# A transformer block on one core: GpSimd's and SP's order inside the attention blocks, and the steps behind the last maximum

## The chip, the core and the metric

The kernel runs on one core of one Trainium2 chip. The metric is the device time of one execution in microseconds (us), taken as the median of three runs. A profile of one execution, with a trace of every instruction, goes with it. TensorE (PE) multiplies matrices, VectorE (DVE), ScalarE (ACT) and GpSimd (POOL) work element by element, and SyncE (SP) only issues transfers; its queue is called SPq in the trace. Each engine takes its own instructions strictly in the order in which they stand, and waits for the others by semaphores.

## The reference

A block of a transformer on 2048 rows of 576 numbers, in float32: layer norm, attention with 32 heads of 18 numbers each, a residual, a second layer norm, a gated feed-forward part with 4608 inner columns, a residual.

```python
qkv = (x_normed @ wqkv).reshape(B, S, 3, H, Dh) ...      # H = 32, Dh = 18
scores = jnp.einsum("bhqd,bhkd->bhqk", q, k) * scale
p = _softmax(scores, axis=-1)
o = jnp.einsum("bhqk,bhkd->bhqd", p, v)
h = x + o.reshape(B, S, D) @ wo
g, u = layernorm(h) @ w_gate, layernorm(h) @ w_up
h2 = h + (gelu(g) * u) @ w_down
```

## The kernel before

Products in float32 accuracy are made of float16 ones: each number is split into a high and a low part, and the products high-high, high-low and low-high are added in PSUM.

**Attention.** The 32 heads are worked in 8 groups of 4 (`NG`), the queries in 4 pieces of 512 (`NB`). A *block* n is one group with one piece of queries, 32 blocks in all (`NS`); n // 4 is the group g and n % 4 the piece qc. A block has 16 *steps* kt, one for each 128 keys. In a step `score` (L704) multiplies 128 keys with 512 queries for the four heads into PSUM banks, ScalarE takes the exponential (L714 for two heads at once, L716 for one), and `weigh` (L725) multiplies the exponentials of the step before with V in two halves of 256 queries, each half called "w". The array is used in tiles of 64 rows by 32 columns: heads 0 and 2 lie in rows 0 to 63, heads 1 and 3 in rows 64 to 127.

**Maxima.** Each query's largest score has to be subtracted before the exponential. `maxima` is a generator that runs one and a half blocks ahead: 64 units a block, each a product of 128 queries with 512 keys (L642), whose maximum VectorE takes (L656, and L654 for pairs of key blocks that are compared by key differences). When a block's 64 units are done and the generator is resumed once more, `max_finish` reduces them (L667), GpSimd scales them and splits them into two parts (L670 to L672), SP transposes these (L674) and writes them as two more rows of the stacked queries Q in four transfers (L680). The scores of that block read Q, and so wait for it.

**Behind a block.** `out_block` has three parts, run at steps of the next block. First (step 0 or 1): ScalarE copies the sums out of PSUM (L739), GpSimd adds the second bank (L742), SP fetches the row sums (rc, L747). Second (step 3): GpSimd makes their reciprocals (L754 to L758), and SP sends them out and back spread over the rows (L762, L763). Third (step 5, or 6 in the last blocks): GpSimd multiplies and splits (L767 to L769), and SP copies the result into the activations X (L782, L785, L786). From block 30 on VectorE does the multiplying.

**Loads.** `load_stacks` brings the next group's queries and keys (L593, L594; 12 transfers on SP, 12 on GpSimd), `load_ends` the keys of which `key_steps` makes the differences (GpSimd L622 to L625, SP L628 and L630). They stand at steps 2 and 9 of a group's first block (of the second block in group 0).

**What sets the order.** The order of the main loop is written out by hand: `STEPS` holds two strings, for even and odd steps, in which "s23" scores heads 2 in bank 3, "S010" heads 0 and 1 in banks 0 and 1, "m4" or "o2" resumes `maxima` once in that bank, "w" weighs a half, and "f" takes a piece of work that is done on the side. `in_order` keeps TensorE, ScalarE, VectorE and GpSimd to the order in which the program issues. SP is not kept to it in the main loop: a scheduler places SP's transfers, until the second `in_order` behind the loop.

**Behind the last maximum.** Maxima end at step 489 of 512 (`LAST_MAX`, block 30, step 9). From there on `STEPS` runs with "m" doing nothing, and each step takes a half of an output product: `wo_pairs` multiplies 128 rows with 288 columns of wo in 14 matmuls (L325, from `accumulate`) into one bank, VectorE adds x and stores the row (L859), whose statistics follow (L213, L214, and GpSimd's L250 to L258). `rows0` makes from pairs of such rows the sums and splits that the feed-forward part multiplies (L261, GpSimd L908 to L911, VectorE L917 to L921), and SP transposes them into X and V (L947). It is taken twice a step from the ninth step on. A third set of 512 rows follows in eight halves, seven of them behind the loop, through four banks; then the first unit of the feed-forward part starts (L1193).

## Time and profile before

| | us |
|---|---|
| median of 3 runs | 2631.65 (2628.14 to 2634.61) |
| the profiled execution | 2628.84 |
| its span in the trace | 2627.1 |
| TensorE busy | 2548.7 (97%) |
| VectorE busy | 2003.7 (76%) |
| ScalarE busy | 1651.6 (63%) |
| GpSimd busy | 858.0 (33%) |

The span is the time from the first to the last instruction; the execution has 1.7 us around it. Busy times are shares of the whole span, in which three stretches follow each other: the preparation to about 200 us, the attention to about 1405 us, the feed-forward part to the end. In a row of the trace stand the start, the duration, the engine, the line, the operation, the tiles written and read with their sizes, the count, and in brackets how long the engine stood idle before and what ended that.

### The profile page before, as it was taken

The numbers are of one execution on the slowest core, as the hardware profiler recorded it, in microseconds if no ns is written. First come the engines' busy times: TensorE is split into PE (matmuls) and PEld (weight loads), VectorE is DVE, ScalarE is ACT, GpSimd is POOL, SyncE is SP. The second block draws the span as 40 slices with busy tenths as digits, with TensorE's granted clock in tenths as the row PEclk, the third lists the DMA queues.
The fourth block names the chain that finished last, engine by engine and source line by source line (L and its number), as shares of the span: only waits on it lengthen the run. The fifth ranks groups of instructions, "written<-read, shape, count | busy, mean of one in ns | idle before, by whom it ended". The sixth has DMA issues, their size and how long they took to land.

```text
span 2627.1 us, 96403 instructions
## 1 busy us (share of the span) xinstructions
PE 2548.7 (97%) x41245; PEld 1446.6 (55%) x41245; DVE 2003.7 (76%) x3888; ACT 1651.6 (63%) x2898; POOL 858.0 (33%) x1176
## 2 busy tenths in 40 slices
PE   8999899999999999999999999999999999999999
PEld 4645455555555555555555555555555555555555
DVE  8479899999999999999957765656565656565653
ACT  6229899999999999999965433333333333333332
POOL 4301532332323232433676432222222222222221
PEclk9999999999999999999999999999999999999999
DMA  8621010101101010101126410101010101011110
GB/s 225 153 78 46 18 47 21 43 19 32 36 18 44 18 47 21 44 20 30 29 59 130 91 34 30 34 30 34 30 34 30 34 30 34 30 33 31 33 56 36
DMA packets 170367, 120.96 MB, mean 46 GB/s; under 512 B 88664, under 2 KB 147564, under 8 KB 169938
## 3 DMA queue, kind: packets, MB, share of 16 engines
q1 hardware_dynamic: 161198, 98.47, 14.0%
q0 software_dynamic: 8608, 16.33, 2.4%
q8 instruction: 322, 5.28, 0.9%
q14 instruction: 107, 0.88, 0.1%
q10 hardware_dynamic: 132, 0.01, 0.0%
HBM read 80.05 MB, written 15.01 MB: 36 GB/s over the span
## 4 chain that ended last, share of the span: by engine, by line
PE 67%; DVE 8%; POOL 7%; issue 5%; SPq 5%; ACT 4%; DMA 4%; ACTq 0%; POOLq 0%; DVEq 0%
PE bank L1193 14%; PE more L1193 14%; PE bank L325 11%; PE more L325 8%; DVE mx L656 6%; PE bank L642 4%; ACT WK L716 3%; PE bank L725 3%; PE quad L725 3%; PE quad L325 2%; DVE nat L654 2%; PE pair L704 2%; POOL rp L754 2%; PE bank L704 1%; SPq L628 1%
## 5 line engine op out<-in xcount | busy, mean ns | idle before, releaser
L656 DVE TENSOR_REDUCE mx<-bank 128x1 f32<-128x512 f32 x1064 | 707.9, 683 | 61.9 <-PE bank L642 60.3
L725 PE MATMUL bank<-WK,V 64*32 64x256 f32 x8192 | 644.8, 383 | 11.0 <-ACT nat L739 10.5
L725 PE MATMUL quad<-WK,V 64*32 64x256 f32 x8192 | 644.2, 383 | 0.2 <-DVE nat L744 0.2
L716 ACT ACTIVATE WK<-bank 128x512 f32<-128x512 f32 x768 | 530.7, 691 | 49.4 <-PE bank L642 33.3
L1193 PEld LDWEIGHTS <-W 128*128 128x128 f16 x2394 | 234.0, 98 | 278.5
L325 PEld LDWEIGHTS <-WK 128*128 128x128 f16 x3456 | 338.2, 98 | 88.3
L716 ACT ACTIVATE WK<-quad 128x512 f32<-128x512 f32 x512 | 355.4, 694 | 16.2 <-PE bank L704 12.7
L656 DVE TENSOR_REDUCE mx<-pair 128x1 f32<-128x512 f32 x488 | 336.8, 690 | 2.9 <-PE pair L642 0.8
L714 ACT ACTIVATE WK<-pair 128x1024 f32<-128x1024 f32 x256 | 279.5, 1092 | 0.4 <-ACT WK L716 0.2
L725 PEld LDWEIGHTS quad<-WK,V 64*32 64x32 f32 x8192 | 239.5, 106 | 29.5 <-DVE nat L744 0.7
L725 PEld LDWEIGHTS bank<-WK,V 64*32 64x32 f32 x8192 | 220.4, 106 | 39.2 <-ACT nat L739 21.4
L325 PE MATMUL more<-W,WK 128*128 128x288 f16 x1728 | 235.2, 286 | 0.0
L325 PE MATMUL bank<-W,WK 128*128 128x288 f16 x1728 | 235.2, 286 | 0.0
L642 PEld LDWEIGHTS <-W 54*32 54x32 f16 x4096 | 139.3, 90 | 171.4 <-issue 111.4
L642 PEld LDWEIGHTS <-A 54*32 54x32 f16 x4096 | 131.7, 90 | 169.8 <-issue 112.5
L1193 PE MATMUL bank<-X,W 128*128 128x512 f16 x792 | 223.8, 379 | 0.0
L642 PE MATMUL bank<-W 54*32 54x512 f16 x2048 | 206.4, 389 | 6.0
L642 PE MATMUL bank<-A 54*32 54x512 f16 x2220 | 205.2, 387 | 6.1 <-DVE mx L656 0.4
L1061 POOL TENSOR_TENSOR A<-A 128x384 f32<-128x384 f32 x136 | 138.5, 1039 | 200.9 <-DMA A<-in_B_w_up_dram 117.1
L1193 PE MATMUL bank<-V,W 128*128 128x512 f16 x720 | 202.4, 379 | 0.0
L1207 POOL TENSOR_TENSOR WK<-tmp,WK 128x512 f16<-128x512 f32 x73 | 88.7, 1215 | 307.5 <-ACT WK L1204 307.2
L716 ACT ACTIVATE WK<-pair 128x512 f32<-128x512 f32 x256 | 178.6, 698 | 0.0
(360 smaller groups left out, 4952.8 us busy)
## 6 DMA issues: line engine op xcount, KB each, us to landing
A<-in_B_w_down_dram SPq DMA_DIRECT2D x8, 1152.0 KB
nat<-rc SPq DMA_DIRECT2D x32, 256.0 KB
A<-in_B_w_gate_dram SPq DMA_DIRECT2D x64, 128.0 KB
A<-in_B_w_up_dram SPq DMA_DIRECT2D x64, 128.0 KB
qk_hi<-tmp SPq DMA_DIRECT2D x36, 128.0 KB
qk_lo<-tmp SPq DMA_DIRECT2D x36, 128.0 KB
out_dram<-nat SPq DMA_DIRECT2D x16, 288.0 KB
X<-nat SPq DMA_DIRECT2D x100, 36.0 KB
```

The source lines that it names most:

```text
L325: nc.tensor.matmul(dst, a, b, start=(i == 0), stop=(i == len(pairs) - 1))
L642: mm = [nc.tensor.matmul(pm[c : c + CT, :TB], Q[r, q0 + c : q0 + c + CT], keys, start=True, stop=True) for c in range(0, P, CT)]
L654: nc.vector.tensor_tensor_reduce(row, pm[:, :TB], row, 1.0, LOWEST, ALU.add, ALU.max, dst)
L656: red = nc.vector.tensor_reduce(dst, pm[:, :TB], axis=AX.X, op=ALU.max)
L704: mm += [nc.tensor.matmul(pS[c : c + CT, :TB], K[r, kt * P + c : kt * P + c + CT], Q[r, qc * TB : (qc + 1) * TB], start=True, stop=True) f ...
L714: act = nc.scalar.activation(pe, pair, AF.Exp, scale=ex_reg)
L716: act = nc.scalar.activation(pe[:, heads[0] % 2], bank_at(bank)[:, :TB], AF.Exp, scale=ex_reg)
L725: nc.tensor.matmul(acc[CT * hh : CT * hh + CT, qs], Vg[n // NB][ks, kt * G4 + hh * VC : kt * G4 + hh * VC + CT], pes[(2 * kt + hh // 2) % ...
L754: nc.gpsimd.tensor_tensor(rc[:, c : c + 4], den[:, c : c + 4], minus_one.to_broadcast([P, 4]), op=ALU.pow)
L1061: op(W8[:, d], W8[:, a], W8[:, b])
L1193: nc.tensor.matmul(bank, w, x_, start=start and i == 0, stop=i == len(mm) - 1, skip_group_check=not start)
L1207: nc.gpsimd.tensor_sub(hl[:, 2 * i + j], v, hh[:, 2 * i + j])
```

## The change

Seven edits:

- In a block the third part of `out_block` moves from step 5 to step 9 (6 in blocks 30 and 31), behind `max_finish`.
- The loads move from step 2 to step 10 of a group's first block, and the key differences from step 9 of that block to step 10 of the next, with their transfers at step 13 (group 0 keeps its loads).
- SP is kept to the program's order from the start of the main loop on.
- From block 30 on VectorE in place of GpSimd scales and splits the maxima, and clears the buffer for block 31.
- Behind the last maximum a list of its own, `LATE`, replaces `STEPS`: the scores of heads 0 and 1, of 2, of 3, a piece of an output product, and both halves' weighing. It holds no "m": `maxima` is not resumed behind its last unit, so `max_finish` is not run for block 31, and its scores are taken with the maxima that block 23, of group 5, left in the same rows of Q. Softmax does not depend on the number that is subtracted.
- The output product is cut after every 11 matmuls (`WO_CUT`) in place of every 14, and its halves use two banks by turns.
- `rows0` makes the sums of an index just before that index is cut, not one ahead, and its pieces are taken at steps that follow from when the rows are ready. The third 512 rows use two banks in place of four.

```diff
@@ max_finish
-        nc.gpsimd.tensor_scalar_mul(m, m, 1 / MSC)
-        nc.gpsimd.tensor_copy(hst[:, :, 0], m)
-        nc.gpsimd.tensor_sub(hst[:, :, 1], m, hst[:, :, 0])
+        by = nc.gpsimd if n < NS - 2 else nc.vector
+        by.tensor_scalar_mul(m, m, 1 / MSC)
+        by.tensor_copy(hst[:, :, 0], m)
+        by.tensor_sub(hst[:, :, 1], m, hst[:, :, 0])
@@ wo_tiles
-                run(accumulate(pt[:, :HALF], products(slice(t * P, (t + 1) * P), oh, ol, ws)))
+                pairs = products(slice(t * P, (t + 1) * P), oh, ol, ws)
+                for j, (a, b) in enumerate(pairs):
+                    nc.tensor.matmul(pt[:, :HALF], a, b, start=(j == 0), stop=(j == len(pairs) - 1))
+                    count += 1
+                    if cut and count % cut == 0 and j + 1 < len(pairs):
+                        yield
@@ rows0
-        yield from sums(0)
         for i in range(TPB):
-            if i + 1 < TPB:
-                yield from sums(i + 1)
+            yield from sums(i)
             yield from cut_rows(i)
@@ the main loop
-    m_ring = ring([singles[2], quads[1], singles[0], singles[1]])
+    m_ring = ring([singles[2], quads[1]])
...
+    LATE = "w S010 s22 s33 L w f w".split()
+    WO_CUT = 11
+    ready = [-(-(i + 1) * 4 * 14 // WO_CUT) for i in range(TPB)]
+    in_order.enter_context(tc.manual_schedule(engines={EngineType.SP}))
...
-            for step in STEPS[kt % 2]:
+            after = n * NT + kt - LAST_MAX
+            for step in LATE[after > 0 :] if after >= 0 else STEPS[kt % 2]:
...
+                elif step == "L":
+                    take(fill)
...
-            if n and kt in ((2 if n == NS - 1 else 3, 6) if late else (3, 5)):
+            if n and kt in (2 if n == NS - 1 else 3, 6 if n > NS - 3 else 9):
                 take(ob)
             if n * NT + kt == LAST_MAX - 2:
-                fill = wo_pairs(ring(singles[:1]))
+                fill = wo_pairs(ring([singles[2], quads[1]]), WO_CUT)
                 take(fill)
-            after = n * NT + kt - LAST_MAX
-            if after >= 0:
-                take(fill)
-            if after >= 8:
-                take(rows, 2)
+            take(rows, sum(2 for r in ready if after + 1 - r in (2, 4, 5, 6)))
             if n == NS - 1 and kt == NT - 2:
                 run(fill)
-                fill = wo_block(2, m_ring)
+                fill = wo_block(2, ring([singles[2], quads[1]]))
                 take(fill)
...
-            if g + 1 < NG and kt == 2 and qc == (1 if g == 0 and NB > 1 else 0):
+            if g + 1 < NG and (qc, kt) == ((1, 2) if g == 0 else (0, 10)):
                 load_stacks(g + 1)
                 load_ends(g + 1)
-            if g + 1 < NG and kt == 9 and qc == (1 if g == 0 and NB > 1 else 0):
-                key_steps(g + 1)
+            if g + 1 < NG and qc == 1 and kt == 10:
+                steps_made = key_steps(g + 1)
+                take(steps_made)
+            if g + 1 < NG and qc == 1 and kt == 13:
+                run(steps_made)
...
-    in_order.enter_context(tc.manual_schedule(engines={EngineType.SP}))
...
-    for _ in fill:
-        take(rows, 2)
+    for i, _ in enumerate(fill):
+        take(rows, 0 if i < 1 else 2)
```

What this makes of the order is seen on three engines. First SP in a block of the middle of a group, before; rc is the row sums and their reciprocals, X<-nat the copies of the output block, mT the transposed maxima:

```order
L747 DMA rc<-nat 128x1x16
L762 DMA rc_862<-rp 128x16
L763 DMA nat<-rc_862 128x1x512
L782 DMA X<-nat 18x2x512 x4
L674 DMA_TRANSPOSE mT<-mm_858 128x1x128
L680 DMA A<-mT 2x4x128 x4
```

And SP in the same place after the change:

```order
L755 DMA rc<-nat 128x1x16
L770 DMA rc_862<-rp 128x16
L771 DMA nat<-rc_862 128x1x512
L676 DMA_TRANSPOSE mT<-mm_858 128x1x128
L682 DMA A<-mT 2x4x128 x4
L790 DMA X<-nat 18x2x512 x4
```

The transpose and its four rows have moved ahead of the four copies. GpSimd in such a block, before; rp and re are the reciprocals, nat the output block, m and mm the maxima and their parts, mx the cleared buffer:

```order
L742 TENSOR_TENSOR nat<-nat 128x512
L754 TENSOR_TENSOR rp<-rc,minus_one 128x4 x4
L756 TENSOR_TENSOR re<-rc,rp 128x16
L757 TENSOR_SCALAR re<-re 128x16
L758 TENSOR_TENSOR rp<-rp,re 128x16
L767 TENSOR_TENSOR nat<-nat 128x512
L768 CAST nat<-nat 128x512
L769 TENSOR_TENSOR nat<-nat 128x512
L670 TENSOR_SCALAR m<-m 128x16
L671 CAST mm_858<-m 128x4x4
L672 TENSOR_TENSOR mm_858<-m,mm_858 128x4x4
L802 MEMSET mx 128x4x2
```

And after:

```order
L750 TENSOR_TENSOR nat<-nat 128x512
L762 TENSOR_TENSOR rp<-rc,minus_one 128x4 x4
L764 TENSOR_TENSOR re<-rc,rp 128x16
L765 TENSOR_SCALAR re<-re 128x16
L766 TENSOR_TENSOR rp<-rp,re 128x16
L672 TENSOR_SCALAR m<-m 128x16
L673 CAST mm_858<-m 128x4x4
L674 TENSOR_TENSOR mm_858<-m,mm_858 128x4x4
L810 MEMSET mx 128x4x2
L775 TENSOR_TENSOR nat<-nat 128x512
L776 CAST nat<-nat 128x512
L777 TENSOR_TENSOR nat<-nat 128x512
```

The three parts of the maxima have moved ahead of the multiplication of the output block. Last VectorE behind the main loop, where the halves of the third 512 rows are read out of their banks and the rows of the last index are cut (CAST into tmp_82 and what follows), before:

```order
L917 CAST tmp_82<-V 128x4x288
L919 TENSOR_TENSOR tmp_82<-V,tmp_82 128x4x256
L920 TENSOR_TENSOR tmp_82<-V,tmp_82 128x4x32
L921 COPY tmp_82<-tmp_82 128x4x32
L859 SCALAR_TENSOR_TENSOR nat<-bank_68,u_o,A 128x288
L917 CAST V<-V 128x2x288
L919 TENSOR_TENSOR V<-V 128x2x256
```

And after:

```order
L875 SCALAR_TENSOR_TENSOR nat<-bank_68,u_o,WK 128x288
L936 CAST tmp_82<-V 128x4x288
L938 TENSOR_TENSOR tmp_82<-V,tmp_82 128x4x256
L939 TENSOR_TENSOR tmp_82<-V,tmp_82 128x4x32
L940 COPY tmp_82<-tmp_82 128x4x32
L875 SCALAR_TENSOR_TENSOR nat<-quad_74,u_o,WK 128x288
```

Before, the last index's first cut stands ahead of the first half's reading (bank_68, x in A); after, it stands behind the third half's (bank_68, x in WK) and ahead of the fourth's (quad_74).

More of the change, by code (lines that the diff above doesn't have):

```diff
@@ L694, in bank_at @@
         return pair[:, i] if i < 2 else (singles[:3] + quads[1:2])[i - 2]
+    weighed = set()
     def score(n, kt, heads, bank):
         g, qc = divmod(n, NB)
+        k2 = n * NT + kt - NPE // 2
+        assert k2 < 0 or {(k2, 0), (k2, 1)} <= weighed
         mm = []
@@ L720, in weigh @@
     def weigh(n, kt, accs, q):
+        weighed.add((n * NT + kt, q))
         qs = slice(q * TB // 2, (q + 1) * TB // 2)
@@ L801, in maxima @@
             if n:
-                nc.gpsimd.memset(mx[:, :, 0, 1::2], LOWEST)
+                (nc.gpsimd if n < NS - 1 else nc.vector).memset(mx[:, :, 0, 1::2], LOWEST)
             for u in range(0, UPS, 2):
@@ L841, in tile_block, with wo_tiles @@
     PIECES = 2 * NK + 9
-    def wo_tiles(ts, ring_, xbs=xbs):
+    rows_made = set()
+    def wo_tiles(ts, ring_, xbs=xbs, cut=None):
         by = ts[1] - ts[0]
+        count = 0
         def fetch(k):
@@ L857, in wo_tiles @@
                 pt = next(ring_)
-                run(accumulate(pt[:, :HALF], products(slice(t * P, (t + 1) * P), oh, ol, ws)))
+                pairs = products(slice(t * P, (t + 1) * P), oh, ol, ws)
[3 more added lines that the diff above has]
+                    if cut and count % cut == 0 and j + 1 < len(pairs):
+                        yield
                 nc.vector.scalar_tensor_tensor(nat[:, t, ws], pt[:, :HALF], u_o, xbs[k % 2][:, ws],
@@ L865, in wo_tiles, with wo_pairs @@
                         rstd_beside(t - by, 2, 256.0, by)
-                yield
+                        rows_made.update((t - by, t))
+                if not cut or count % cut == 0:
+                    yield
     def wo_block(b, ring_, xbs=xbs):
         return wo_tiles(list(range(b * TPB, (b + 1) * TPB)), ring_, xbs)
-    def wo_pairs(ring_):
-        return wo_tiles([t for i in range(TPB) for t in (i, TPB + i)], ring_)
+    def wo_pairs(ring_, cut):
+        return wo_tiles([t for i in range(TPB) for t in (i, TPB + i)], ring_, cut=cut)
     VP = view(V, 0, (2 * PIECES, TB), F16)
@@ L904, in sums @@
             y2, y1 = (F.rearrange("p a b -> p (a b)")[:, k * D : (k + 1) * D] for k in range(2))
+            assert {i, TPB + i} <= rows_made
             normed(y1, nat[:, i], i)
@@ L1308, in tile_block @@
     load_ends(0)
-    key_steps(0)
+    run(key_steps(0))
     load_w(of, wo, nc.gpsimd)
```

## The prediction

> **What bounds the kernel now.** I read the page first, then the stretches of the run, then who waited for whom, and last one wait in order of time. The page's first rows give the busy time of each engine and its share in 40 slices of 66 us.
>
> ```profile
> PE 2548.7 (97%) x41245; PEld 1446.6 (55%) x41245; DVE 2003.7 (76%) x3888; ACT 1651.6 (63%) x2898; POOL 858.0 (33%) x1176
> DVE  8479899999999999999957765656565656565653
> ACT  6229899999999999999965433333333333333332
> ```
>
> Slices 4 to 20 are the attention: VectorE and ScalarE both stand at 9 there. After it they fall, and TensorE alone stays full. The shares of the whole run hide this, so I ask for stretches. Each row gives the stretch, its length, then the busy time of PE, PEld, DVE, ACT and POOL, the granted clock, and the DMA share. A block is one n (512 queries of four heads, 16 steps); the edges are the copies at L739 that close a block.
>
> ```profile
> 242.50:1309.20 1066.70, 1010.63 (x29692) 563.86 (x29692) 1019.70 (x1927) 1028.53 (x1886) 394.56 (x603) 0.98 0.12 31
> 685.90:726.60 40.70, 35.56 (x1020) 19.60 (x1020) 35.09 (x66) 35.85 (x67) 9.68 (x15) 0.93 0.09 21
> 762.00:797.30 35.30, 34.51 (x1032) 19.41 (x1024) 35.06 (x67) 35.30 (x67) 9.67 (x15) 1.00 0.11 29
> ```
>
> An undisturbed block takes 35.3 us, and ScalarE is busy for all of it (35.30 of 35.30): it bounds the block. The first row holds 29 blocks. The block from 685.90 has the same work and takes 40.70 us, and nothing is busy in the difference. The waits of TensorE in the attention say why:
>
> ```profile
> PE bank L704 <- DMA A<-mT: 17.0, 7, 6.3
> PE bank L704 <- DMA W<-mT: 16.7, 7, 4.0
> ```
>
> That is 33.7 us in 14 waits for the transposed maxima of the next block, the longest 6.3 us. One of them in order of time, from VectorE's last reduction over GpSimd and the DMA queue of SP to TensorE:
>
> ```profile
> 703.01 0.22 DVE L667 TENSOR_REDUCE m<-mx 128x16 f32<-128x64 f32 x1
> 704.82 0.58 SPq L763 DMA_DIRECT2D nat<-rc  x1
> 709.93 1.28 POOL L767 TENSOR_TENSOR nat<-nat 128x512 f32<-128x512 f32 x1 [8.05 <-DMA nat<-rc]
> 713.21 0.26 POOL L670 TENSOR_SCALAR m<-m 128x16 f32<-128x16 f32 x1
> 713.15 4.12 SPq L782 DMA_DIRECT2D X<-nat  x5
> 717.38 1.14 SPq L674 DMA_TRANSPOSE mT<-mm  x1
> 719.67 2.75 SPq L680 DMA_DIRECT2D W<-mT  x4
> 722.83 0.61 PE L704 MATMUL bank<-W 56*32 56x512 f16 x4 [4.00 <-DMA W<-mT]
> ```
>
> The maxima are ready at 703.2. GpSimd stands 8.05 us on the output block's multiplication, whose reciprocals are still on the way, and takes the maxima's parts up at 713.2. SP then puts five copies of the output ahead of the transpose. From the transpose to the first score go 5.45 us (722.83 - 717.38).
>
> **The change, part by part.** *Parts and loads in the blocks.* The multiplication moves from step 5 to step 9 of a block, behind the maxima's parts (step 8); the loads move to step 10, the key differences to a block later. SP now runs in the written order: rc, its two transfers, the transpose, the four rows, and only then the copies. In the example GpSimd would start the parts at about 703.3; with the three parts (0.8 us) and 5.45 us the scores could start at 709.6. They want to at 718.8 (722.83 - 4.00), so 9 us are to spare, and all 14 waits should go. What is late next is ScalarE. Two estimates of the gain: 29 undisturbed blocks of 35.35 are 1025.2, so 1066.7 - 1025.2 = 41.5; ScalarE's own busy time leaves 1066.7 - 1028.5 = 38.2. I take 40. Least is 33.7, the waits alone.
>
> What the moved loads and key differences meet is priced by a row of SP, seven transfers of key differences at 0.92 us:
>
> ```profile
> 276.20 6.42 SPq L628 DMA_DIRECT2D kd<-nat  x7
> ```
>
> Twenty loads from step 10 on take at most 18 us, 8 steps of 2.2, and end at step 2 of the next block; eleven transfers of key differences from step 13 on take 10 us and end there too. The row sums' transfer rc, due at step 1, comes a step late in these blocks, and its reciprocals (about 6 us with the landing) at step 5: before the parts at step 8, so this costs nothing. The cover is 3 steps, 6 us; beyond it the transpose is late.
>
> Of the gain above the waits, a part is the slow stretch behind a wait:
>
> ```profile
> 540.09 0.56 PE L704 MATMUL bank<-A 56*32 56x512 f16 x4 [1.77 <-DMA A<-mT]
> 540.00:543.60 3.60, 3.51 (x72) 2.06 (x77) 2.08 (x4) 2.56 (x4) 0.00 (x0) 0.53 0.06 13
> ```
>
> The first row is a block's first score behind a wait of 1.77 us; the stretch behind it has a granted clock of 0.53. The Trainium skill ("TensorE: Matmul & The Clock Gate", part 1) gives half rate to TensorE after an idle window of about 3.4 us; here a wait of half that length did it. By that rule nearly all waits would cost only themselves, some 34 us together; the block lengths above are measured and decide.
>
> *The maxima's parts on VectorE from block 30 on, and the dropped last ones.* Four small operations of about 0.2 us (by the L667 row) on an engine that is busy for 35.06 of 35.3 us: +0.8, at least nothing. The step list behind the last maximum holds no "m", so the maxima of block 31 are not finished or transposed (31 transposes in place of 32); they were off the path, so 0.
>
> *The steps behind the last maximum.* The stretch before, from there to the last weighing, in two pieces; then TensorE's rows over two steps (14 matmuls are one half of an output product):
>
> ```profile
> 1327.30:1390.30 63.00, 60.47 (x1042) 34.47 (x1046) 29.70 (x71) 34.61 (x61) 44.28 (x80) 1.00 0.31 76
> 1390.30:1402.40 12.10, 11.82 (x301) 6.08 (x286) 9.51 (x22) 12.10 (x23) 8.02 (x16) 1.00 0.76 141
> 1383.08 1.89 PE L325 MATMUL bank<-W,X 128*128 128x288 f16 x14
> 1384.92 0.59 PE L704 MATMUL pair<-W 56*32 56x512 f16 x8
> 1386.06 0.40 PE L704 MATMUL bank<-W 56*32 56x512 f16 x4
> 1386.39 1.89 PE L325 MATMUL bank<-W,X 128*128 128x288 f16 x14
> 1388.21 0.42 PE L725 MATMUL bank<-WK,V 64*32 64x256 f32 x4
> 1388.66 0.40 PE L704 MATMUL quad<-W 56*32 56x512 f16 x4
> 1390.29 0.40 PE L704 MATMUL bank<-W 56*32 56x512 f16 x4
> 1406.92 5.31 PE L325 MATMUL bank<-W,X 128*128 128x288 f16 x42
> ```
>
> Sixteen steps with a half each take 63.0 us and leave TensorE as the bound. The six steps without one take 12.1 us, 2.0 each, and ScalarE is the bound (12.10 of 12.10). So TensorE's products are crowded into 16 steps, and the change spreads them over 20.4 (224 matmuls by 11). A matmul of a half costs (5.31 - 0.17)/42 = 0.1224 us, so 11 cost 1.35 and 14 cost 1.71. The rest of a step is (1390.29 - 1383.08 - 2 x 1.71)/2 = 1.9 us before: two halves of weighing of 0.45 each (1388.21 to 1388.66), and scores. The new order puts heads 2 and 3 side by side: they lie in different halves of the array's rows, and eight such matmuls of heads 0 and 1 ran in 0.59 us where four took 0.40. So I put the rest at 1.73, between 1.45 and 2.0. Steps: 20 x 3.08 = 61.6; step 20 with the last four matmuls 2.2; step 21 2.0; step 22 with the first half of the next rows 3.4; last weighing 0.9: 70.1 us. Before it is 1405.2 - 1327.3 = 77.9. Gain 7.8, from 1.5 to 14.
>
> The drained array between product and scores costs some of it: 1386.06 to 1386.39 for four scores that take half of that beside others. The Trainium skill ("TensorEngine Tiling", Key Properties) has every change of the tiling mode drain TensorE, which speaks against cutting the product finer. By it the four added pieces would cost some 1.3 us; the 1.73 above has this in it.
>
> *The first rows of x.* They are now fetched in the written order, behind the copies of block 29:
>
> ```profile
> 1326.27 1.63 SPq L785 DMA_DIRECT2D X<-nat  x2
> 1332.59 0.70 SPq L786 DMA_DIRECT2D X<-nat  x1
> 1344.40 0.36 SPq L849 DMA_DIRECT2D A<-in_A_x_dram  x1
> 1347.27 0.52 DVE L859 SCALAR_TENSOR_TENSOR nat<-bank,u_o,A 128x288 f32<-128x288 f32 x1 [3.92 <-DMA A<-in_A_x_dram]
> ```
>
> The copies end 6.0 us behind the stretch's start (1333.3), and a fetch takes 2.9 us to its reader, so VectorE reads the first bank at +9.4 instead of +3.8. Two banks hold 28 matmuls, 2.55 steps, +7.9: TensorE waits 1.6 us (0 to 3).
>
> *The tail.* The rows of index 3 are now cut behind the loop, among the last seven halves of the third 512 rows, which go through two banks instead of four.
>
> ```profile
> 1385.44 1.09 DVE L917 CAST tmp<-V 128x1152 f16<-128x1152 f32 x1
> 1386.56 1.70 DVE L919 TENSOR_TENSOR tmp<-V,tmp 128x1024 f16<-128x1024 f32 x1
> 1407.10 2.77 SPq L947 DMA_TRANSPOSE X<-tmp  x2
> 1412.75 1.51 SPq L947 DMA_TRANSPOSE V<-V  x1
> 1417.21 1.03 PE L1193 MATMUL more<-X,A 128*128 128x512 f16 x4
> ```
>
> Call the loop's end E (1405.2 before). Before, the first product of the feed-forward part starts at E + 12.0, and the last transposes are issued by E + 9.1. Now VectorE reads half 3 until E + 4.0 and cuts until E + 7.3 (1.09 + 1.70 + 0.5), so half 4's bank is read at E + 7.8; half 6 wants it at E + 6.9. Half 7 waits in the same way behind the second cut, 1.3 us. The products end at E + 14.2, and three transposes of 1.4 us issued from E + 7.3, with about 3 us to land, come at the same time. So +2.5 (0 to 6).
>
> Sum: -40 + 0.8 - 7.8 + 1.6 + 2.5 = -42.9. The profiled execution took 2628.84 us (span 2627.1), which gives 2585.9; the median of the runs lies 2.8 higher, which gives 2588.7. I forecast 2588. The ends, from the median: -41.5 - 14 gives 2576; -33.7 + 0.8 - 1.5 + 3 + 6 = -25.4 gives 2606.
>
> **The rivals.** *Part of the waits stays* (0.17): GpSimd is still held before the parts, by the pieces of the output weight in block 2 and the loads in every fourth block. With half of the gain gone, -20 - 3 gives 2609. For it speaks the longest wait, in front of which such a piece stood:
>
> ```profile
> 308.09 1.73 POOL L827 TENSOR_SCALAR nat<-nat,p_s_wo 128x576 f32<-128x576 f32 x1
> 318.29 0.62 PE L704 MATMUL bank<-A 56*32 56x512 f16 x4 [6.32 <-DMA A<-mT]
> ```
>
> Against it speak the 9 us to spare, more than a few pieces of under 2 us.
>
> *The tail takes the late gain back* (0.12): the cut rows come 8 us later than the products end, TensorE waits, and 2597 is left.
>
> *The late steps run at their floor and the tail is hidden* (0.07): 2576.
>
> *Slower* (0.04): SP in written order holds the transpose behind nat<-rc, which waits for the reciprocals. If these come late in every block, every block waits. In the example nat<-rc is issued by 705.4; the transpose may start until 713.4 (718.8 - 5.45), 10.4 us behind the reduction, without harm. Each us more costs 31 us over 31 blocks. The 33.7 us of waits now and the 8 us won late are used up at 1.35 us a block, that is from 11.8 us on; at 13 us it is 31 x 2.6 - 41.7 = 39 us slower, 2670.
>
> **How the numbers follow.** The forecast's case has 0.59, with 2579 to 2597 as its own range. With the floor case and the tail case inside, the range 2574 to 2607 leaves out the slower case and the worse half of the case in which waits stay. A measurement here cannot tell less than 0.3% (8 us) from no change. Faster by more than that: 0.59 + 0.17 + 0.12 + 0.07 = 0.95, less 0.01 for waits that nearly all stay: 0.94. Within it: 0.02. Slower: 0.04.
>
> **What would show it.** Right: no waits of TensorE for mT, blocks of 35.3 to 35.5 us throughout, ScalarE full in them, the transpose ahead of the copies on SP, steps of about 3.1 us behind the last maximum, a stretch of 70 us there, and the first feed-forward product some 14 us behind the loop. Wrong: waits for mT that remain, or blocks over 36 us without such a wait, or late steps above 3.4 us.

## The result, and the profile after

| | before | after |
|---|---|---|
| median of 4 runs, us | 2630.95 (2628.14 to 2634.61) | 2592.22 (2589.48 to 2595.18) |
| span of the profiled execution, us | 2627.1 | 2590.7 |

The ratio is 0.9852, with a 95% interval from 0.9835 to 0.9869. That is 38.7 us faster, inside the forecast's range and 4 us above the forecast time. In spans, in which the sum was made, 42.9 us were forecast and 36.4 came. The terms stray further than the sum does: one was too small on the good side, two were too small on the bad side.

The stretches of the kernel after, with the same columns and edges as before: 29 blocks of attention, the last block among them (block 29), the steps behind the last maximum, and the tail from the second half of the third 512 rows to the first product of the feed-forward part.

```profile
242.80:1270.40 1027.60, 999.33 (x29704) 561.09 (x29696) 1019.34 (x1932) 1024.74 (x1886) 394.08 (x599) 1.00 0.13 33
1233.40:1270.40 37.00, 35.04 (x1032) 19.22 (x1027) 36.78 (x73) 35.68 (x66) 31.51 (x32) 1.00 0.14 36
...
1287.66:1360.18 72.52, 68.71 (x1376) 40.47 (x1374) 35.57 (x91) 46.88 (x71) 46.73 (x88) 0.98 0.50 100
1360.18:1380.08 19.90, 12.82 (x107) 9.58 (x100) 12.94 (x33) 0.59 (x1) 7.37 (x16) 1.00 0.54 123
```

The 29 blocks take 1027.6 us instead of 1066.7, at full clock, and ScalarE is busy for 1024.7 of them: it is the bound in all blocks now but block 29, where VectorE is busy for 36.78 of 37.00. The late stretch fell only from 77.9 to 72.5 us, and the tail grew from 12.0 to 19.9. Next, TensorE's waits from the first block to the tail, those that a transfer or VectorE ended:

```profile
PE bank L871 <- DVE nat L875: 6.5, 3, 3.6
PE more L1210 <- DVE nat L875: 3.0, 1, 3.0
PE bank L710 <- DVE mx L657: 1.8, 3, 1.1
PE quad L871 <- DVE nat L875: 1.1, 1, 1.1
```

No wait for mT is left. What is new are 10.6 us of waits for VectorE's reading of the output products (L875). The largest entry of that view is not new: weighing (L733) waits 13.1 us in 27 short waits for ScalarE's copy at the end of a block, 10.2 us in 20 before. One block in order of time shows why the waits for mT went:

```profile
684.44 0.22 DVE L668 TENSOR_REDUCE m<-mx 128x16 f32<-128x64 f32 x1
684.75 0.26 POOL L672 TENSOR_SCALAR m<-m 128x16 f32<-128x16 f32 x1 [4.31 <-DVE m L668]
685.61 1.14 SPq L676 DMA_TRANSPOSE mT<-mm  x1
687.26 1.28 POOL L775 TENSOR_TENSOR nat<-nat 128x512 f32<-128x512 f32 x1 [1.63 <-DMA nat<-rc]
692.92 4.16 SPq L790 DMA_DIRECT2D X<-nat  x5
```

GpSimd stands idle when the reduction ends and takes the parts at once; the transpose leaves 1.2 us behind the reduction (685.61 - 684.44) instead of 14.4 in the block shown before (717.38 - 703.01). The multiplication follows, and the copies come last on SP. GpSimd still waits for the reciprocals, 1.63 us, but nothing urgent stands behind it.

The late waits come from transfers. First the output product that waits longest:

```profile
1293.91 0.70 SPq L794 DMA_DIRECT2D X<-nat  x1
1294.85 0.34 SPq L860 DMA_DIRECT2D A<-in_A_x_dram  x1
1298.29 0.52 DVE L875 SCALAR_TENSOR_TENSOR nat<-bank,u_o,A 128x288 f32<-128x288 f32 x1 [10.61 <-DMA A<-in_A_x_dram]
1298.86 1.36 PE L871 MATMUL bank<-W,X 128*128 128x288 f16 x5 [3.65 <-DVE nat L875]
```

SP issues the last copy of block 29, then the first rows of x; VectorE gets them 3.4 us later, and TensorE has been without a bank for 3.65 us. Then the tail, SP's transposes and fetches with their readers:

```profile
1356.12 2.89 SPq L964 DMA_TRANSPOSE V<-V  x2
1359.06 0.58 SPq L860 DMA_DIRECT2D A<-in_A_x_dram  x1
1363.56 0.52 DVE L875 SCALAR_TENSOR_TENSOR nat<-bank,u_o,A 128x288 f32<-128x288 f32 x1 [7.16 <-DMA A<-in_A_x_dram]
1364.13 1.88 PE L871 MATMUL bank<-W,X 128*128 128x288 f16 x14 [2.06 <-DVE nat L875]
...
1374.53 1.53 SPq L860 DMA_DIRECT2D WK<-in_A_x_dram  x1
1379.08 0.52 DVE L875 SCALAR_TENSOR_TENSOR nat<-bank,u_o,WK 128x288 f32<-128x288 f32 x1 [3.38 <-DMA WK<-in_A_x_dram]
1380.08 2.57 PE L1210 MATMUL more<-X,A 128*128 128x512 f16 x7 [2.98 <-DVE nat L875]
```

The first half's bank is full at 1358.4 (1356.47 and 1.89 us), but its row of x stands behind the transposes of the cut rows on SP, and the bank is read only at 1363.56. The last one comes in the same way behind the transposes of the last cut rows. The bank of the last half is one that the feed-forward part's first product takes over, so that product waits too.

Term by term, in us (start of the late stretch: 1327.3 before, 1287.66 after):

| | forecast | measured |
|---|---|---|
| attention up to the late stretch, with the parts on VectorE | -39.2 | -39.6 |
| late steps without the wait for x (67.15 in fetch_first) | -7.8 | -10.7 |
| wait for the first rows of x (72.52 - 67.15) | +1.6 | +5.4 |
| tail | +2.5 | +7.9 |
| behind it (1209.9 before, 1210.6 after) | 0 | +0.7 |
| sum | -42.9 | -36.4 |

### The profile page after: what moved, and what is told of

Read it like the earlier page. It is cut to its first block, busy times and chain, and to the rows that moved or that the text cites. A ratio compares the mean times of both kernels' runs of the same rounds, so it can differ in the third digit from the quotient of the medians.

```text
span 2590.7 us, 96377 instructions
## 1 busy us (share of the span) xinstructions
PE 2532.7 (98%) x41245; PEld 1442.9 (56%) x41245; DVE 2000.1 (77%) x3891; ACT 1647.7 (64%) x2886; POOL 852.6 (33%) x1169
## 4 chain that ended last, share of the span: by engine, by line
PE 73%; DVE 14%; ACT 6%; issue 4%; DMA 2%; SPq 0%; POOL 0%; ACTq 0%; DVEq 0%; POOLq 0%
PE bank L1210 15%; PE more L1210 15%; PE bank L325 10%; DVE mx L657 10%; PE more L325 8%; PE bank L643 6%; ACT WK L722 4%; PE bank L733 4%; PE quad L733 4%; DVE nat L655 3%; PE quad L325 2%; PE pair L710 2%; PE bank L710 2%; PE pair L325 1%; PE quad L643 1%
## 5 line engine op out<-in xcount | busy, mean ns | idle before, releaser
L733 PE MATMUL bank<-WK,V 64*32 64x256 f32 x8192 | 631.8, 379 | 13.2 <-ACT nat L747 13.1
L733 PE MATMUL quad<-WK,V 64*32 64x256 f32 x8192 | 634.1, 380 | 0.0
L722 ACT ACTIVATE WK<-bank 128x512 f32<-128x512 f32 x780 | 538.5, 694 | 1.0 <-PE bank L710 1.0
L722 ACT ACTIVATE WK<-quad 128x512 f32<-128x512 f32 x488 | 341.7, 700 | 1.6 <-PE quad L710 1.3
L720 ACT ACTIVATE WK<-pair 128x1024 f32<-128x1024 f32 x268 | 293.1, 1094 | 23.9 <-PE pair L710 22.6
L733 PEld LDWEIGHTS quad<-WK,V 64*32 64x32 f32 x8192 | 236.0, 106 | 24.5 <-DVE nat L749 0.3
L733 PEld LDWEIGHTS bank<-WK,V 64*32 64x32 f32 x8192 | 217.1, 105 | 37.6 <-ACT nat L747 21.8
L1228 ACT COPY tmp<-more 128x512 f32<-128x512 f32 x36 | 21.0, 583 | 243.7 <-PE more L1210 186.4
```

The costliest lines, as they stand in the source:

```text
L720: act = nc.scalar.activation(pe, pair, AF.Exp, scale=ex_reg)
L722: act = nc.scalar.activation(pe[:, heads[0] % 2], bank_at(bank)[:, :TB], AF.Exp, scale=ex_reg)
L733: nc.tensor.matmul(acc[CT * hh : CT * hh + CT, qs], Vg[n // NB][ks, kt * G4 + hh * VC : kt * G4 + hh * VC + CT], pes[(2 * kt + hh // 2) % ...
L1228: nc.scalar.copy(xg, g[0])
```

## The experiments

The theory after the result: the attention's gain comes from GpSimd's order; the late steps gained over 10 us, and SP's written order gave most of that back, since fetches of x came to stand behind copies and transposes. The rivals: SP's order made the attention's gain; the late steps are worth little; the two banks or VectorE's cuts make the tail long whatever the fetches do. All runs in one table; the last three columns are the stretches of the profiled execution, by the same edges as above, in us. The runs stand in batches, each with the kernel before beside it: its median was 2628.55 for att_alone to sp_free, 2626.41 for fetch_first to fetch_both_4 and 2626.46 for the last four. So medians are compared inside a batch, and ratios across batches.

| run | median | ratio to before (95%) | 29 blocks | late | tail |
|---|---|---|---|---|---|
| before | 2630.95 | | 1066.7 | 77.9 | 12.0 |
| after | 2592.22 | 0.9852 (0.9835 to 0.9869) | 1027.6 | 72.5 | 19.9 |
| att_alone | 2602.38 | 0.9903 (0.9886 to 0.9919) | 1030.1 | 84.7 | 17.0 |
| late_alone | 2624.05 | 0.9981 (0.9970 to 0.9992) | 1062.5 | 67.5 | 15.2 |
| mul_step5 | 2638.25 | 1.0035 (1.0022 to 1.0047) | 1076.5 | 73.6 | 20.8 |
| sp_free | 2589.15 | 0.9853 (0.9837 to 0.9870) | 1036.3 | 67.6 | 15.4 |
| fetch_first | 2584.68 | 0.9839 (0.9826 to 0.9853) | 1027.7 | 67.2 | 18.6 |
| fetch_queue | 2582.28 | 0.9832 (0.9819 to 0.9846) | 1029.8 | 73.2 | 13.8 |
| four_banks | 2587.66 | 0.9854 (0.9839 to 0.9869) | 1029.6 | 70.4 | 13.8 |
| fetch_both_4 | 2578.03 | 0.9815 (0.9801 to 0.9828) | 1028.3 | 67.2 | 12.6 |
| apart_4 | 2577.20 | 0.9816 (0.9799 to 0.9832) | 1028.0 | 66.6 | 12.4 |
| cut14_4 | 2583.89 | 0.9846 (0.9830 to 0.9862) | 1029.2 | 70.2 | 14.2 |
| parts_pool_4 | 2578.10 | 0.9818 (0.9801 to 0.9834) | 1029.2 | 67.2 | 12.1 |
| finish31_4 | 2576.62 | 0.9813 (0.9797 to 0.9829) | 1028.7 | 67.2 | 12.4 |

**att_alone: the attention part without the late part.** The kernel before with these edits; the loads and key differences are moved and the last maxima's parts taken by VectorE as in the change (not shown here):

```diff
+    in_order.enter_context(tc.manual_schedule(engines={EngineType.SP}))
     for n in range(NS):
...
-            if n and kt in ((2 if n == NS - 1 else 3, 6) if late else (3, 5)):
+            if n and kt in (2 if n == NS - 1 else 3, 6 if n > NS - 3 else 9):
```

> The kernel before with the attention part of the change alone: the multiplication at step 9, the loads at step 10, the key differences a block later, SP in written order from the first block on; the steps behind the last maximum, the output products and the tail stay as before. Theory (the gain of 39 us lies in the attention, and the late part of the change gave its own gain back): no waits for mT, 29 blocks in 1027 to 1030 us (1066.7 before), the late stretch 5 to 8 us longer than before (77.9) because the first rows of x stand behind the copies here too and one bank holds only 14 matmuls of cover, tail as before (12.0 us): 2598 (2594 to 2602). Rival (the late part of the change gains its 8 us and something else ate them): 2592 - 39 share, that is 2588 to 2593 with the late stretch at 77.9.

The tail of this kernel:

```profile
1373.81:1390.81 17.00, 13.71 (x106) 10.24 (x99) 8.07 (x24) 0.58 (x1) 1.89 (x7) 0.90 0.70 139
```

The attention keeps its gain (1030.1 us for the 29 blocks), so that part needs nothing of the late edits. The late stretch is 84.7 us, 6.8 longer than before, as the theory had it. The tail was expected at 12.0 and took 17.0 with before's own four banks: the first sign that the written order costs there too. The time, 2602.4, is just above the theory's band for that reason.

**late_alone: the late part without the attention part.** The kernel after with the attention's edits undone and SP free until behind the loop.

```diff
-    in_order.enter_context(tc.manual_schedule(engines={EngineType.SP}))
     for n in range(NS):
...
-            if n and kt in (2 if n == NS - 1 else 3, 6 if n > NS - 3 else 9):
+            if n and kt in ((2 if n == NS - 1 else 3, 6) if late else (3, 5)):
```

> The kernel after with its attention part undone: multiplication at step 5, loads and key differences at their old steps, SP free until behind the loop; own step list behind the last maximum, pieces of 11 matmuls, two banks, rows behind them. Theory: the attention as before (1066.7 us, waits for mT), the late stretch 66 to 69 us (no wait for the first rows of x), the tail 15 to 20 us instead of 12.0, because its last half lies in a bank that the first product of the feed-forward part waits for: together 3 to 8 us faster than before, 2623 to 2628. Rival (late part worth nothing by itself, tail takes all of it): 2629 to 2633, stretch and tail together 89.9 us or more.

The late stretch takes 67.5 us and the tail 15.2, 82.7 together against 89.9 before. So the late part does pay, by 7 us in the trace and by some 5 us (0.19%, interval 0.08 to 0.30%) over its runs, which lie between 2615.99 and 2629.12; the profiled one is the shortest. The theory's band, 2623 to 2628, held. Alone the two parts gain 26 and 5 us, together they gain 38.7. A part of the difference is seen: in att_alone one bank, not two, stands between the late rows of x and TensorE, which makes its late stretch the longest of all runs. The rest is left open, since late_alone's runs spread over 13 us.

**mul_step5: GpSimd's order undone.**

```diff
-            if n and kt in (2 if n == NS - 1 else 3, 6 if n > NS - 3 else 9):
+            if n and kt in (2 if n == NS - 1 else 3, 6 if n > NS - 3 else 5):
```

> The kernel after with the multiplication back at step 5 of a block, ahead of the maxima's parts; SP stays in written order, which here puts the copies of the output ahead of the transpose. Theory (GpSimd's order carries the gain): waits for mT return, 20 to 40 us of them with the slow clock behind some, 2612 to 2632. Rival (the moved loads and key differences, not the multiplication, removed the waits): no more than 5 us of waits, 2590 to 2597.

A block of this kernel, in order of time:

```profile
752.22 1.29 POOL L775 TENSOR_TENSOR nat<-nat 128x512 f32<-128x512 f32 x1 [8.65 <-DMA nat<-rc]
755.50 0.26 POOL L672 TENSOR_SCALAR m<-m 128x16 f32<-128x16 f32 x1
755.45 4.12 SPq L790 DMA_DIRECT2D X<-nat  x5
759.68 1.14 SPq L676 DMA_TRANSPOSE mT<-mm  x1
765.13 0.40 PE L710 MATMUL bank<-W 56*32 56x512 f16 x4 [3.73 <-DMA W<-mT]
```

It is the chain of the kernel before again: GpSimd held 8.65 us, copies ahead of the transpose, TensorE waiting. The waits for mT are 39.6 us in 14 (22.4 and 17.2), and with SP in written order the kernel is slower than before. The time, 2638.25, lies above the theory's band too: the 29 blocks are 48.9 us longer than in after, 9 us more than the waits (the profiled run is the slowest of six). Under SP's written order, moving the loads and key differences alone removes none of the waits; the place of the multiplication carries the gain. Whether the multiplication could do it with the loads left at their old steps was not run.

**sp_free: SP's order undone.** The line goes back to its old place behind the loop.

```diff
-    in_order.enter_context(tc.manual_schedule(engines={EngineType.SP}))
     for n in range(NS):
...
+    in_order.enter_context(tc.manual_schedule(engines={EngineType.SP}))
     run(side)
```

> The kernel after with SP scheduled by the builder until behind the loop, as before; all steps of the generators stay where the change put them. Theory (the order on GpSimd is what freed the transposes, SP's written order is not needed): 29 blocks within 1027 to 1033 us, no wait for mT over 1 us, and the first rows of x come no later than in after: 2586 to 2594. Rival (SP's written order was needed to put the transpose ahead of the copies): waits for mT of 10 us or more in all, 2602 or more.

The theory held for the time, and missed in the attention: 1036.3 us, and one long wait for mT. All blocks but one are as in after, without SP's written order. In one place the scheduler puts block 28's copies ahead of the transpose of block 30's maxima:

```profile
1268.37 0.70 SPq L794 DMA_DIRECT2D X<-nat  x1
1269.17 1.12 SPq L676 DMA_TRANSPOSE mT<-mm  x1
...
1274.61 0.61 PE L710 MATMUL bank<-W 56*32 56x512 f16 x4 [8.10 <-DMA W<-mT]
```

That wait of 8.1 us is why the 29 blocks take 1036.3. On the other side the late stretch is 67.6 (72.5 in after) and the tail 15.4 (19.9), because the scheduler issues the fetches of x earlier (the first at 1158.45, against 1294.85 in after). So the written order of SP wins 8.7 us in one block and loses 9.4 us behind the attention (4.9 and 4.5): alone, nothing.

**fetch_first, fetch_queue, four_banks: the late losses one by one.**

```diff
 fetch_first
-            if n * NT + kt == LAST_MAX - 2:
+            if n * NT + kt == LAST_MAX - 4:
 fetch_queue
-                nc.sync.dma_start(xbs[k % 2], xv[:, ts[k]])
+                queue.dma_start(xbs[k % 2], xv[:, ts[k]])
...
-                fill = wo_block(2, ring([singles[2], quads[1]]))
+                fill = wo_block(2, ring([singles[2], quads[1]]), queue=nc.scalar)
 four_banks
-                fill = wo_block(2, ring([singles[2], quads[1]]))
+                fill = wo_block(2, ring([singles[2], quads[1], singles[0], singles[1]]))
```

> The kernel after with the first two rows of x fetched two steps earlier, ahead of the copies of block 29 on SP. Theory (the wait of 3.65 us and the slow clock behind it come from that fetch alone): no wait of TensorE there, the late stretch 67.2 us instead of 72.5 (the pair of scores comes 8.13 us behind the one before it instead of 2.91, so 5.2 us), tail unchanged at 19.9: 5 us faster than after, 2587. Rival (the second bank or VectorE's other work holds the first halves anyway): the wait stays above 2 us, 2591 to 2593.

> The kernel after with the rows of x of the third 512 queries fetched from ScalarE's queue instead of SP's. Theory (the tail waits for these rows, which stand behind the transposes of the cut rows on SP): the first reading by VectorE comes at about 1358.5 instead of 1363.6, the last one at once behind its product instead of at 1379.1; tail 13 to 15 us instead of 19.9: 5 to 7 us faster than after, 2585 to 2587. Rival (two banks and VectorE's cuts set the tail): tail 18 us or more, 2590 to 2592.

> The kernel after with four banks instead of two for the products of the third 512 rows; fetches as in after. Theory (late rows of x set the tail, and two banks turn this into waits): the waits of 2.1, 1.1 and 0.8 us inside the products go, and the last half no longer lies in a bank that the first product of the feed-forward part takes over, so the 3.0 us go too and the cut rows set the end: tail 14 to 17 us instead of 19.9, 3 to 6 us faster, 2586 to 2589. Rival (two banks don't matter, only the fetches do): tail 19 us or more, 2591.

The stretch that each of the three was made for; first fetch_first's late stretch, then the tails of fetch_queue and of four_banks:

```profile
1286.40:1353.55 67.15, 66.98 (x1375) 40.02 (x1374) 36.71 (x89) 46.86 (x71) 48.44 (x88) 1.00 0.49 101
```

```profile
1362.22:1375.97 13.75, 12.34 (x107) 9.60 (x99) 11.38 (x31) 0.59 (x1) 6.85 (x16) 1.00 0.92 155
```

```profile
1358.88:1372.71 13.83, 12.18 (x106) 9.60 (x99) 11.04 (x28) 0.59 (x1) 6.16 (x10) 1.00 0.44 110
```

The three mechanisms hold. With the first fetch ahead of the copies the late stretch is 67.15, as worked out, and TensorE is busy for 66.98 of it. With the third rows of x on ScalarE's queue the tail is 13.75; a wait of 0.80 us at the seventh half (index 6) and one of 0.61 us before the first feed-forward product are all that two banks cost by themselves. With four banks and late fetches the tail is 13.83: the products run through, but two waits of 1.66 and 1.96 us come before and inside the first feed-forward product. So it takes both, late rows of x and only two banks, to make this stretch 6 us longer, and either cure shortens it. They are not worth the same: of four_banks' two waits the second, 1.96 us, lies behind the edge of the tail. From the start of the tail to the end of the program after takes 1230.5 us, four_banks 1226.2 and fetch_queue 1222.7. And att_alone, with before's four banks, still has a tail of 17.0 us, where the first of these rows is issued 4.7 us behind the stretch's start (1378.48 - 1373.81) and not 1.6 us ahead of it as in four_banks (1357.32 against 1358.88). In times, by the ratio, fetch_first and fetch_queue gain some 3 and 5 us on after, with intervals that overlap its own, and four_banks (0.9854 against 0.9852) shows no gain.

**fetch_both_4: all three edits of above in one kernel.**

> The kernel after with all three: the first rows of x two steps earlier, those of the third 512 rows from ScalarE's queue, four banks for their products. Theory: late stretch 67.2 us (72.5 in after), tail 12.5 to 14.5 us (19.9 in after), 11 us faster than after: 2581 (2578 to 2584). Rival (the gains overlap, because what ends later in the tail is the transposes of the cut rows, which keep their distance to the loop's end): tail 17 us or more, 2584 to 2588.

```profile
1354.32:1366.93 12.61, 12.17 (x106) 9.53 (x99) 11.88 (x32) 0.59 (x1) 6.78 (x16) 1.00 0.98 159
```

The late stretch is 67.16 us; this row is the tail. The kernel beats both others: 0.9815 (0.9801 to 0.9828) against 0.9852 (0.9835 to 0.9869) for after. The stretches add up to 79.8 us, where after has 92.4 and before 89.9. The median, 2578, is 3 us better than the theory's middle. What ends last in the tail is now a transpose of the cut rows: TensorE waits 0.44 us for it at 1366.93.

**apart_4 and cut14_4: why a late step is 2.9 us.** Both start from fetch_both_4.

```diff
 apart_4
-    LATE = "w S010 s22 s33 L w f w".split()
+    LATE = "w S010 s22 L s33 w f w".split()
 cut14_4
-    WO_CUT = 11
+    WO_CUT = 14
```

> fetch_both_4 with heads 2 and 3 of the steps behind the last maximum kept apart (scores of head 2, output product, scores of head 3). Theory (the steps came out shorter than forecast, 2.91 us, because the four scores of head 3 run beside those of head 2 and cost no time of their own): each of the 20 steps is 0.2 to 0.35 us longer, the late stretch 4 to 7 us longer, 2582 to 2585. Rival (the scores of head 3 hide behind the product just as well, the pieces of 11 made the gain): stretch within 1.5 us of fetch_both_4, 2577 to 2580.

> fetch_both_4 with a whole half (14 matmuls) in each of 16 late steps and none in the last ones, instead of 11 matmuls in 20. Theory (TensorE's work is the same, and only the few steps without a product, bound by ScalarE at 2.0 us, lose what TensorE idles in them, 0.44 us each): stretch 1 to 2.5 us longer, 2579 to 2581. Rival (spreading the products over all steps was the main gain of the late part): stretch 5 to 8 us longer, 2583 to 2586.

Parting heads 2 and 3 costs nothing (66.58 against 67.16 us): the theory on that step fell. In apart_4 TensorE's rows around head 3 are these:

```profile
1318.35 0.40 PE L710 MATMUL bank<-W 56*32 56x512 f16 x4
1318.37 0.42 PE L733 MATMUL bank<-WK,V 64*32 64x256 f32 x4
```

Behind the output product the four scores start at 1318.35 and the first weighing at 1318.37, beside them. So heads 2 and 3 need not stand together: four scores were hidden here by the weighing that followed them in the other half of the array's rows as well as by head 2's, and cost their own 0.33 us where an output product followed (1386.06 to 1386.39 in the kernel before). The rival had the time right, with another reason: they hide beside the weighing, not behind the product.

In cut14_4 a step with 14 matmuls is 3.27 us (1316.44 to 1319.71), one without is 1.90 (1343.71 to 1345.61, two starts of pair scores), the first of these 1.61 (from 1342.10):

```profile
1298.23 0.42 PE L871 MATMUL bank<-W,X 128*128 128x288 f16 x2 [1.04 <-DMA X<-nat]
...
1316.09 0.42 PE L710 MATMUL bank<-W 56*32 56x512 f16 x8
1316.44 1.89 PE L871 MATMUL bank<-W,X 128*128 128x288 f16 x14
1318.26 0.42 PE L733 MATMUL bank<-WK,V 64*32 64x256 f32 x4
...
1319.71 1.89 PE L871 MATMUL quad<-W,X 128*128 128x288 f16 x14
...
1342.32 0.42 PE L710 MATMUL bank<-W 56*32 56x512 f16 x8
1342.53 0.40 PE L733 MATMUL bank<-WK,V 64*32 64x256 f32 x4
...
1343.71 0.41 PE L710 MATMUL pair<-W 56*32 56x512 f16 x8
...
1345.61 0.56 PE L710 MATMUL pair<-W 56*32 56x512 f16 x8
```

The rest of a step is 3.27 - 14 x 0.1224 = 1.56 us, the same as with 11 matmuls (2.91 - 1.35). So crowding the products costs only the idle TensorE in six steps without a product, five at 1.90 and one at 1.61: 5 x (1.90 - 1.56) + 0.05 = 1.7 us, inside the theory's bounds. The stretch as a whole grew by 3.1 us and left them: about 1.2 us are a wait that neither theory had, where the products reach rows whose attention output is still being copied (1.04 us in the first row). The time, 2583.9, fits the rival, but not for its reason: its 5 to 8 us in the stretch did not come, and 1.6 us of the 5.9 lie in the tail.

**parts_pool_4 and finish31_4: the small edits.** Both start from fetch_both_4; the first keeps the maxima's parts on GpSimd in all blocks, the second finishes the maxima of block 31 as before does.

```diff
 parts_pool_4
-        by = nc.gpsimd if n < NS - 2 else nc.vector
+        by = nc.gpsimd
 finish31_4
             halves += [(n, kt, accs, q) for q in range(2)]
+            if after == 1:
+                take(mxs)
```

> fetch_both_4 with the maxima's parts on GpSimd in all blocks, block 30 too. Theory (the wait of 1.14 us at 1252 to 1254 and a block 29 of 37.1 us come from the four parts in VectorE's queue): the wait goes, block 29 takes 35.4 us, 1.5 us faster, 2576.5. Rival (the block is long for another reason, GpSimd being behind with the feed-forward weights there): a wait for mT of over 1 us in its place, 2578 to 2582.

> fetch_both_4 with the maxima of block 31 finished and transposed as in before, which the change leaves out. Theory (off the path: one reduction, three parts and a transpose beside the first late steps): within 1 us of fetch_both_4, 2577 to 2579. Rival (the transpose and its rows on SP hold the fetches of x, or the scores of block 31 wait for the rows): a wait of TensorE of 2 us or more in the late stretch, 2580 to 2584.

On GpSimd the parts stand behind the splitting of feed-forward weights, and the wait moves rather than goes. The wait in parts_pool_4, then the one in fetch_both_4:

```profile
1268.90 0.40 PE L710 MATMUL bank<-W 56*32 56x512 f16 x4 [1.52 <-DMA W<-mT]
```

```profile
1252.17 0.40 PE L710 MATMUL bank<-W 56*32 56x512 f16 x4 [1.14 <-DVE mx L657]
```

The rival was right; VectorE and GpSimd are about equal there (block 29 takes 37.0 and 37.5 us). Finishing the dropped maxima costs nothing (67.15 us and 12.4 us), so leaving them out bought nothing: there is no gain in time to set against scores that rely on the maxima of another block.

## Why the prediction was right, and where it was not

**The attention: right in mechanism and size.** -39.2 us forecast with the parts, -39.6 measured. All 14 waits went; mul_step5 shows that all come back when one multiplication stands where it stood on GpSimd. The blocks came out at 35.2 to 35.7 us, but for two of 36.1 and 37.1, which is one of the prediction's own signs of being wrong, on 2 blocks of 29; and ScalarE's busy time (1024.7 of 1027.6) is the bound that was named as next. The slower rival had SP's written order hold the transpose behind the reciprocals; it did not, the transpose left 1.2 us behind the reduction. That rival was close at hand all the same: with the multiplication four steps earlier the written order makes the kernel 0.35% slower than before.

**The parts on VectorE: +0.8 forecast; block 29 is 37.1 us.** TensorE waits 1.14 us there for VectorE, which takes the four parts in between its maxima. The alternative is no better.

**The late steps: direction right, term too small, reason partly wrong.** 20 steps at 3.08 us were forecast, 2.91 came; the rest of a step is 1.56 instead of 1.73. The forecast put the saving down to heads 2 and 3 side by side; apart_4 shows that the weighing serves as well. It also took the steps before for shorter than they are: it counted 1383.08 to 1390.29 as two steps, but the next product at the same place of the order starts 7.50 us behind the last, which is 3.75 a step and a rest of 2.04, not 1.9. The row ahead of those in the prediction:

```profile
1375.58 1.89 PE L325 MATMUL bank<-W,X 128*128 128x288 f16 x14
```

Spreading the products, named as the gain, is worth 1.7 us; the shorter step is the larger share, (3.75 - 3.27) x 16 = 7.7 us of the 10.7. That the order inside the step makes it shorter is read from these rows; no run changes the order alone, and a second bank came with it.

What the drained array costs was priced about right. By cut14_4's rows the product of 14 holds TensorE for 1.82 us (1316.44 to 1318.26), 0.11 more than 14 x 0.1224, and the eight scores ahead of it take 0.35 us (1316.09 to 1316.44) where eight ahead of weighing take 0.21 (1342.32 to 1342.53). Together that is 0.25 us a piece, 1.0 for the four added pieces; the prediction's estimate was 1.3. The Trainium skill ("TensorEngine Tiling", Key Properties) says that a change of the tiling mode drains TensorE, and these rows agree.

**The first rows of x: mechanism right, size wrong.** +1.6 forecast, +5.4 measured. VectorE read the first bank at +10.6 us of the stretch (1298.29 - 1287.66) where +9.4 was forecast, and TensorE had used up both banks at +7.5 (1298.86 - 3.65 - 1287.66) rather than +7.9, since the steps were shorter. That makes a wait of 3.65 us. The other 1.7 us are the slow clock behind it, which this row shows in the column before the last two:

```profile
1298.80:1302.20 3.40, 3.34 (x45) 1.61 (x52) 1.37 (x5) 0.00 (x0) 3.25 (x3) 0.50 0.30 87
```

The forecast had priced the slow clock in the blocks and left it out here.

**The tail: a queue left out.** +2.5 forecast, +7.9 measured. What was priced came out somewhat smaller: fetch_queue, with the rows of x out of the way, has a tail of 13.75, +1.7, with no wait at the sixth half, where 0.9 us was worked out, and 0.80 at the seventh, where 1.3 was; the first cut was done at E + 6.4 (1368.61 - 1362.22) and not E + 7.3. What failed is the step "VectorE reads half 3 until E + 4.0": it took the rows of x for the third 512 rows as being at hand. SP's written order was followed for the first rows of x and not for these, whose fetches stand behind the transposes of the cut rows in the same queue. VectorE read the first half at E + 3.4 (1363.56 - 1360.18) and the last two from E + 18.9 on. With two banks, 6 us of the 7.9 are that. The rival in which the tail takes the late gain back described the place and the size, but for another cause, cut rows that come late; with after's 19.9 us against fetch_queue's 13.75, where only the queue of these fetches differs, the late fetches are shown to be the cause.

The errors partly cancelled: -2.9 from the steps against +3.8 and +5.4 from the two fetches. The attention's term rests on a mechanism that the runs show; that the sum came within 6.5 us of the forecast, with three of its smaller terms off by 3 to 5 us, is in part luck.

## What to carry to other kernels

When a queue is put into written order, list every transfer on it to the end of that region and ask what each now stands behind: the order that frees one transpose delays each fetch that is issued late in the program. Where an engine takes its work in order, work that waits for a slow round trip belongs behind work that others wait for; one multiplication four steps later was worth some 48 us here (a ratio of 0.9852 against 1.0035 in mul_step5). A ring of two banks is enough only as long as what empties the banks is never late.

## What the runs showed that was not expected

The same wait costs 3.3 us or 6.0 us, depending on when it falls. In four_banks and in fetch_queue TensorE waits 3.12 us at the same instruction; here the wait, and then TensorE's busy time (the first number behind the length) and the clock in windows of 3.41 us, first in four_banks:

```profile
1299.11 0.77 PE L871 MATMUL bank<-W,X 128*128 128x288 f16 x5 [3.12 <-DVE nat L875]
```

```profile
1293.85:1297.26 3.41, 2.14 (x54) 1.19 (x39) 0.00 (x0) 2.29 (x4) 3.31 (x3) 1.00 0.52 141
1297.26:1300.67 3.41, 1.56 (x37) 1.01 (x44) 1.88 (x5) 0.00 (x0) 3.15 (x4) 1.00 0.44 134
1300.67:1304.09 3.42, 3.42 (x86) 1.91 (x67) 0.52 (x1) 2.00 (x3) 3.19 (x4) 1.00 0.27 84
```

The same of fetch_queue:

```profile
1299.72 1.36 PE L871 MATMUL bank<-W,X 128*128 128x288 f16 x5 [3.12 <-DVE nat L875]
```

```profile
1295.31:1298.72 3.41, 1.29 (x25) 0.60 (x7) 0.00 (x0) 2.00 (x3) 3.25 (x3) 1.00 0.63 187
1298.72:1302.14 3.42, 2.42 (x29) 1.21 (x36) 1.88 (x5) 0.00 (x0) 3.19 (x3) 0.50 0.34 96
1302.14:1305.55 3.41, 3.41 (x40) 1.57 (x25) 0.00 (x0) 2.00 (x3) 3.15 (x4) 0.50 0.07 22
```

In every trace here the granted clock changes only on a grid of 3.41 us. Whether it stays full in the next window goes by how long TensorE was idle in this one. In the fourteen traces, from 200 to 2570 us, all windows with up to 1.4 us of idle time kept the clock and all with 1.9 or more lost it. Between these both occur: 1.47 in fetch_queue (window from 203.05) and 1.77 in before (from 536.78) lost it, 1.85 in fetch_first (from 1368.19) kept it. In four_banks the grid splits the wait into 1.27 and 1.85 us, and the clock stays; the late stretch is 70.4 us, 3.3 above fetch_first. In fetch_queue 2.12 us of idle time fall into one window, the clock is halved for two, and the stretch is 73.2, 6.0 above. The Trainium skill ("TensorE: Matmul & The Clock Gate", part 1) has a free-running window of this length, and the traces agree; it speaks of an idle window, where here about half a window was enough.
